# Four interleaved attention layers: projections on two row halves that swap PSUM banks, activations turned by DMA, A's queries read from PSUM, x by way of DRAM

## The chip, the cores and the metric

One core of one Trainium2 chip runs the whole program. The metric is device time in microseconds of one execution; the times shown are three executions and their median. The engines of the core run their own queues in order: TensorE (PE, with its weight loads PEld), VectorE (DVE), ScalarE (ACT), GpSimd (POOL) and SyncE (SP), which here only issues DMAs.

## What is computed

A sequence of 2048 rows of 512 numbers goes through four attention layers, A, B, A, B, each with its residual:

```python
x = x + A(layernorm(x)); x = x + B(layernorm(x))
x = x + A(layernorm(x)); x = x + B(layernorm(x))
```

Both layers have 32 heads of 16 numbers, a projection to queries, keys and values (512 to 1536) and an output projection (512 to 512). In A each row attends to 8 keys, its own and those 2, 4, ... 14 rows before. In B each row attends to the 256 rows that end with its own. Softmax is over these keys, with scale 1/4. Everything is float32 in and out.

## The kernel before

**Tiling.** Rows are cut into 8 chunks of 256. For each pair of layers and each chunk, `layer_a` and `layer_b` plan all work of that chunk; the scopes A0 to A15 and B0 to B15 number them (8 chunks, two pairs of layers).

**Numbers.** Projections multiply float32 values as two float16 parts, high and low: every product is three matmuls (high by high, high by low, low by high), on full 128-row tiles, accumulated in float32 in PSUM. `norm` computes mean and variance on DVE, the reciprocal root on POOL, the normalized rows `xn` on ACT; PE turns them by four transposes into the tile `pt`, ACT copies the high part `xh` and DVE subtracts it for the low part `xl`. `proj_t` makes a turned result of 512 by 256 (q and k of both layers, v of A) in two PSUM tiles, one after the other; `proj_n` makes an unturned one (v of B, both output projections), one tile of 128 rows at a time.

**A.** ACT copies q from PSUM to SBUF; DVE (and POOL for some) multiplies it with the shifted keys into `pr`; PE sums over the 16 numbers of a head by a 0/1 matrix, as column tiles, into `L`; softmax in `e`; PE spreads the probabilities over the numbers of a head by `selt`, on 32 rows, into `pb`; DVE multiplies with the values into `pw`, POOL or DVE sums.

**B.** The high and low parts of q and k go through DRAM (`re`) into the stacked tiles `stk`, where a 48-row slice holds one head's three products. `sq` are the scores for the row maxima, `m`; the maxima are split in two float16 parts, turned by PE (`pm`), copied, and put by DMA into two further rows of `stk`, so that `sk`, on 64 rows, gives scores less the maximum. ACT takes the exponential into `p`, POOL masks, PE multiplies with the values as column tiles into `av`; sums, reciprocals and the result's new layout go through DMAs (`os`, `rc`, `scr`, `oc`).

**Memory.** PSUM has two pools: `q_sc`, two tiles of two banks for scores, and `q_pj`, four banks for everything else. The rows x of a chunk stay in SBUF (`px`, three buffers) from A's load to the end of B.

**The order.** Nothing runs in the order of the calls. `plan.add(engine, us, fn, r, w, mode, ...)` records a task; `ORDER[scope]` gives, for each task of a scope in order of recording, its place in the queue of its engine, all scopes together. A negative entry -1-p means place p on the task's other engine (`alt`). `Plan.order` then merges the five queues by the planned costs and writes the program. So the engines' orders are written out in full, and every engine waits at the head of its own queue. `IDLE` tasks (three matmuls without use) stand in PE's order where the plan expects it to run empty.

Of the kernel before, what the change touches and what calls it, by code (L numbers as in the profile page):

```python
# [9 lines left out]
F16 = mybir.dt.float16  # L10
# [8 lines left out]
P = 128  # L19
# [339 lines left out]
}  # L359
IDLE = 110  # L360
LAG = {"PE": 0.23, "DVE": 0.13, "ACT": 0.16, "POOL": 0.1, "SP": 0.0}
RATE = 0.33
SLOW = 0.25
# [165 lines left out]
def kernel(  # L529
# [193 lines left out]

    x_dr = {}
    vx_dr = {}
    x_in = {}
    st8 = {}


    def norm(l, c):  # L730
# [15 lines left out]
        def rstd():  # L746
            nc.gpsimd.tensor_tensor(out=rs.t[:, 0], in0=rs.t[:, 0], in1=mhalf, op=ALU.pow)
# [602 lines left out]
```

## Time and profile before

| | |
|---|---|
| runs | 1522.99, 1513.79, 1518.68 us; median 1518.68 us |
| span of the profiled execution | 1515.1 us; no other time of it is given |
| PE busy, by modelled ends | 1394.5 us, 92% |
| DVE busy | 1257.6 us, 83% |
| ACT busy | 732.5 us, 48% |
| POOL busy | 695.4 us, 46% |
| mean granted clock of PE | 0.959 |
| bytes moved by DMA | 96.34 MB |

The span runs from the first to the last instruction of the execution that was profiled. A group's row gives line, engine, operation, output and inputs with their shapes and count, then busy time in us and the mean of one in ns, then the engine's idle time before them and what ended it. Matmuls overlap, so their durations are longer than their distance; a row of the timeline with its start time shows the distance.

### The profile page before, as it was taken

The numbers are of one execution on the slowest core, as the hardware profiler recorded it, in microseconds if no ns is written. First come the engines' busy times: TensorE is split into PE (matmuls) and PEld (weight loads), VectorE is DVE, ScalarE is ACT, GpSimd is POOL, SyncE is SP. The second block draws the span as 40 slices with busy tenths as digits, with TensorE's granted clock in tenths as the row PEclk, the third lists the DMA queues.
The fourth block names the chain that finished last, engine by engine and source line by source line (L and its number), as shares of the span: only waits on it lengthen the run. The fifth ranks groups of instructions, "written<-read, shape, count | busy, mean of one in ns | idle before, by whom it ended". The sixth has DMA issues, their size and how long they took to land.

```text
span 1515.1 us, 35124 instructions
## 1 busy us (share of the span) xinstructions
PE 1394.5 (92%) x14186; PEld 793.1 (52%) x14186; DVE 1257.6 (83%) x2361; ACT 732.5 (48%) x1011; POOL 695.4 (46%) x783
## 2 busy tenths in 40 slices
PE   6899989989898998989999998999989899898988
PEld 4574636546374553736446363645637365463544
DVE  6968797987979888897988869798897979889774
ACT  6522445455455554455545344544544555445554
POOL 2504163463726356172452727255372735628232
PEclk9898989999999998999999898998999999999999
DMA  6030211222121221222112122212212121121221
GB/s 236 15 97 23 69 47 56 56 61 75 41 87 37 70 56 53 78 52 77 45 52 77 39 87 52 84 38 60 79 41 85 33 88 48 57 77 40 77 53 44
DMA packets 73091, 96.34 MB, mean 64 GB/s; under 512 B 17120, under 2 KB 44256, under 8 KB 72928
## 3 DMA queue, kind: packets, MB, share of 16 engines
q1 hardware_dynamic: 72672, 93.83, 21.5%
q8 instruction: 111, 1.82, 0.5%
q14 instruction: 52, 0.43, 0.1%
q10 hardware_dynamic: 256, 0.26, 0.1%
HBM read 49.81 MB, written 34.05 MB: 55 GB/s over the span
## 4 chain that ended last, share of the span: by engine, by line
PE 56%; DVE 19%; POOL 7%; issue 6%; ACT 5%; DMA 4%; SPq 3%; ACTq 0%; POOLq 0%; DVEq 0%
PE pq L792 9%; PE pq L793 7%; PE pq L794 7%; PE av L1201 6%; DVE m L1117 5%; PE sk L1169 4%; ACT p L1175 4%; PE L L929 3%; DVE sq L1115 3%; PE po L811 3%; PE sq L1096 3%; PE po L813 2%; PE po L812 2%; POOL pw L1008 2%; PE sq L1099 2%
## 5 line engine op out<-in xcount | busy, mean ns | idle before, releaser
L1175 ACT ACTIVATE p<-sk,sclB 128x768 f32<-128x768 f32 x480 | 426.6, 900 | 297.5 <-PE sk L1171 278.3
L1184 POOL TENSOR_SCALAR_AFFINE_SELECT p<-p 128x1024 f32<-128x1024 f32 x240 | 266.6, 1116 | 499.4 <-ACT p L1175 455.5
L1117 DVE TENSOR_REDUCE m<-sq 128x2 f32<-128x512 f32 x448 | 310.4, 693 | 15.4
L1115 DVE COPY_PREDICATED sq<-maskt,sq 128x256 f32<-128x256 int16 x448 | 188.8, 421 | 81.4 <-PE sq L1099 74.7
L1201 PE MATMUL av<-p,v 128*32 128x128 f32 (+1 forms) x3840 | 202.6, 334 | 7.4 <-POOL p L1184 7.3
L921 DVE TENSOR_TENSOR pr<-kv,q 128x512 f32<-128x512 f32 x223 | 167.4, 807 | 35.4 <-ACT q L900 17.1
L1169 PE MATMUL sk<-stk,stk 64*128 64x256 f16 x960 | 138.2, 287 | 36.8 <-DVE m L1117 20.2
L1201 PEld LDWEIGHTS av<-p,v 128*32 128x32 f32 x3840 | 109.0, 110 | 93.7 <-issue 33.3
L1001 DVE TENSOR_TENSOR pw<-pb,kv 128x1024 f32<-128x1024 f32 x128 | 153.1, 1214 | 4.0 <-POOL o L1010 1.7
L1008 POOL TENSOR_TENSOR pw<-pw 128x512 f32<-128x512 f32 x104 | 132.7, 1276 | 25.1 <-DVE pw L1001 24.4
L1096 PE MATMUL sq<-stk,stk 48*128 48x128 f16 (+1 forms) x896 | 114.5, 255 | 32.0 <-DVE m L1117 17.8
L1099 PE MATMUL sq<-stk,stk 48*128 48x256 f16 (+1 forms) x1024 | 128.4, 252 | 8.5 <-DVE m L1110 3.6
L1169 PEld LDWEIGHTS <-stk 64*128 64x128 f16 x960 | 53.3, 94 | 156.4 <-issue 99.4
L1096 PEld LDWEIGHTS <-stk 48*128 48x128 f16 x896 | 50.0, 95 | 123.1 <-issue 78.8
L1171 PE MATMUL sk<-stk,stk 64*128 64x128 f16 x960 | 109.3, 223 | 0.0
L763 ACT ACTIVATE xn<-x,rs 128x512 f32<-128x512 f32 x64 | 52.0, 813 | 80.9 <-DVE rs L750 72.9
L1009 POOL TENSOR_TENSOR pw<-pw 128x256 f32<-128x256 f32 x104 | 76.3, 734 | 8.2
L921 POOL TENSOR_TENSOR pr<-kv,q 128x512 f32<-128x512 f32 x33 | 46.5, 1415 | 58.7 <-PE L L929 36.0
L929 PE MATMUL L<-pr,sel 128*32 128x512 f32 x512 | 70.6, 601 | 0.9 <-DVE pr L921 0.7
L792 PE MATMUL pq<-xh,wA0h 128*128 128x256 f16 x256 | 70.9, 277 | 0.4 <-DVE el L1032 0.4
L792 PE MATMUL pq<-xh,wB0h 128*128 128x256 f16 x256 | 70.2, 274 | 1.0 <-DVE el L1032 1.0
L792 PE MATMUL pq<-xh,wA2h 128*128 128x256 f16 x256 | 70.6, 276 | 0.0
(183 smaller groups left out, 3159.9 us busy)
## 6 DMA issues: line engine op xcount, KB each, us to landing
stk<-re SPq DMA_DIRECT2D x256, 96.0 KB
re<-eh SPq DMA_DIRECT2D x128, 128.0 KB
re<-el SPq DMA_DIRECT2D x64, 128.0 KB
oc<-os SPq DMA_DIRECT2D x120, 64.0 KB
os<-scr SPq DMA_DIRECT2D x15, 512.0 KB
x<-in_A_x_dram SPq DMA_DIRECT2D x8, 512.0 KB
xd<-x SPq DMA_DIRECT2D x16, 256.0 KB
x<-xd SPq DMA_DIRECT2D x8, 512.0 KB
```

The costliest lines, as they stand in the source:

```text
L792: nc.tensor.matmul(ps[mp].t[:, i], wh, xh, start=k == 0, stop=False)
L921: E.tensor_mul(pr.t, window(kv[1].t, m, 64 * tq, 64)[:, 0], qb)
L1001: nc.vector.tensor_mul(pw.t, pb.t.unsqueeze(1).broadcast_to([P, 2, W, 64]), v)
L1008: E.tensor_add(t[:, :, 0:4], t[:, :, 0:4], t[:, :, 4:8])
L1096: nc.tensor.matmul(ps.t[:, par, 0 : (2 - qb) * P], lhs, stk[hf, bef][r, col, qb * P :], start=True, stop=True)
L1099: nc.tensor.matmul(ps.t[:, par, (2 - qb) * P : 3 * P], lhs, stk[hf, now][r, col, : (1 + qb) * P], start=True, stop=True)
L1115: nc.vector.copy_predicated(t[:, :, 0:P], maskt[:, 0:P].bitcast(I16).unsqueeze(1).broadcast_to([P, 2, P]), t[:, :, 2 * P : 3 * P])
L1117: nc.vector.tensor_reduce(out=m.t[:, qb, :, u], in_=t[:, :, 0 : 2 * P], op=ALU.max, axis=AX.X)
L1169: nc.tensor.matmul(o[:, two], k[:, jf * P : (jf + 1) * P], q, start=True, stop=True)
L1175: nc.scalar.activation(pt.t[:, :, 2 * i : 2 * i + 2].rearrange("p s m q -> p m s q"), ps.t[:, :, : 3 * P].rearrange("p m (s q) -> p m s q" ...
L1184: nc.gpsimd.affine_select(out=v, in_=v, pattern=[[0, 8], [-1 if b == 0 else 1, P]], compare_op=ALU.is_gt if b == 0 else ALU.is_ge, fill=0. ...
L1201: nc.tensor.matmul(o, v[:, jj, 17 * h : 17 * h + 32], rhs, start=z == 0 and (b == 0 or first), stop=z == 1 and b == 1, tile_position=(0, 3 ...
```

## The change

- **Projections.** Each matmul over 128 rows becomes two over 64, on the array's upper and lower row half, which write two different PSUM tiles. In a first turn tile 0 takes the upper rows and tile 1 the lower; in a second turn they swap. Between the turns a task on SP, a no-op, waits for the last matmul of the first turn, and the first matmul of the second waits for the no-op (`turn_over`, `turns`). Both tiles of a projection are in use for both turns. There are 8 projections for each of 16 chunk pairs.
- **Turning.** The high part `hi` is taken by ACT from `xn` in SBUF, the low part by POOL or DVE; both are turned by DMA transposes, issued on SP, into `xh` and `xl`. The transposes on PE, their PSUM tiles, and the copies from them go. `rstd` on POOL takes over the small steps of the norm from DVE.
- **A's queries** are not copied; DVE reads them in PSUM. POOL, which doesn't read PSUM here, makes no products any more.
- **A's spreading** matmuls take 64 rows instead of 32, with zeros in `selt` for the other 32.
- **Row maxima of B** are turned as float32 on the two row halves into a tile of `q_sc` (before: split first, turned whole, in `q_pj`); ACT writes the high part, DVE the low.
- **B's values** are accumulated in one tile for each half of a head group, with a copy to SBUF for each.
- **x** is stored to DRAM at the end of A and loaded again for the end of B.
- **ORDER** is new for all scopes, and 16 idle tasks are left of 110.

```diff
 def norm(l, c):
     def stats(t):
         nc.vector.bn_stats(b6.t[:, t], xb.t[:, t])
         nc.vector.bn_aggr(mv.t[:, t], b6.t[:, t])
-        nc.vector.tensor_scalar(rs.t[:, 0, t : t + 1], mv.t[:, t, 1:2], 1.0e-5, 1.0 / (XS * XS), ...)
     def rstd():
+        nc.gpsimd.tensor_scalar(rs.t[:, 0], mv.t[:, :, 1], 1.0e-5, 1.0 / (XS * XS), ...)
         nc.gpsimd.tensor_tensor(out=rs.t[:, 0], in0=rs.t[:, 0], in1=mhalf, op=ALU.pow)
-    def shift():
-        nc.vector.scalar_tensor_tensor(rs.t[:, 1], mv.t[:, :, 0], -1.0, rs.t[:, 0], ...)
+        for t in range(2):
+            nc.gpsimd.tensor_scalar(rs.t[:, 1, t : t + 1], mv.t[:, t, 0:1], rs.t[:, 0, t : t + 1], -1.0, ...)
...
-            plan.add("PE", 0.48, transp, r=[vxn], w=[vpt], mode="F", act=0.213)
-            plan.add("ACT", 0.48, ... nc.scalar.copy(xh.t[:, :, sl], pts.t), r=[vpt], w=[vh])
-            plan.add("DVE", 0.61, ... nc.vector.tensor_sub(xl.t[:, :, sl], pts.t, xh.t[:, :, sl]), ...)
+            def rest(E, xn=xn, hi=hi):
+                E.tensor_tensor(out=xn.t.bitcast(F16)[:, 0:D], in0=xn.t, in1=hi.t, op=ALU.subtract)
+            def turn_h(t=t, hi=hi):
+                nc.sync.dma_start_transpose(xh.t[:, :, t * P : (t + 1) * P], hi.t)
+            def turn_l(t=t, xn=xn):
+                nc.sync.dma_start_transpose(xl.t[:, :, t * P : (t + 1) * P], xn.t.bitcast(F16)[:, 0:D])
+            plan.add("ACT", 0.52, lambda xn=xn, hi=hi: nc.scalar.copy(hi.t, xn.t), r=[vxn], w=[vhi])
+            plan.add("SP", 0.1, turn_h, r=[vhi], w=[vh], size=200)
+            plan.add("POOL", 1.12, rest, r=[vxn, vhi], w=[vlo], mode="S", alt=("DVE", 0.6))
+            plan.add("SP", 0.1, turn_l, r=[vlo], w=[vl], size=200)
+    def turn_over(last, wait, chain):
+        def pause():
+            n = nc.sync.nop(nofuse=True)
+            tc.add_manual_dep(n.ins, last[0].ins.name, SYNC)
+            wait.append(n)
+        v = Val()
+        plan.add("SP", 0.15, pause, r=chain, w=[v])
+        return v
+    def turns(last, wait, ins):
+        if wait:
+            tc.add_manual_dep(ins.ins, wait.pop().ins.name, SYNC)
+        last[:] = [ins]
 def proj_t(l, c, s):
-    def part(mp, i, kk):
-        m = 2 * mp + i
+    def part(turn, i, kk):
         for k in kk:
...
-            nc.tensor.matmul(ps[mp].t[:, i], wh, xh, start=k == 0, stop=False)
-            nc.tensor.matmul(ps[mp].t[:, i], wh, xl, start=False, stop=False)
-            nc.tensor.matmul(ps[mp].t[:, i], wl, xh, start=False, stop=k == 3)
+            for n in range(3):
+                for mp in ((0, 1) if turn == 0 else (1, 0)):
+                    half = (mp + turn) % 2
+                    r = slice(64 * half, 64 * half + 64)
+                    w = wt[T, s, "l" if n == 2 else "h"][r, k]
...
+                    x = d["xl" if n == 1 else "xh"].t[r, k]
+                    turns(last, wait, nc.tensor.matmul(ps[mp].t[:, i], w, x, ...))
...
+    for turn in range(2):
...
+                    plan.add("PE", 0.655, lambda turn=turn, i=i, kk=kk: part(turn, i, kk), act=0.64,
+                             r=[*d["vxt"], vwt[T, s], *chain], w=[*vps, nxt], mode="R")
...
+        if not turn:
+            chain.append(turn_over(last, wait, chain))
 def finish(l, c, o, vo):
+    if T == "B":
+        mid, vmid = x_mid[c]
+        xb = buf("px", [P, 2, D], F32, "x", f"xr{l}_{c}")
+        plan.add("SP", 0.5, lambda: nc.sync.dma_start(xb.t, mid.t.rearrange("(t p) d -> p t d", p=P)), ...)
...
+    if T == "A":
+        plan.add("SP", 0.4, lambda t=t, mid=x_mid[c][0]: nc.sync.dma_start(mid.t[t * P : (t + 1) * P], xb.t[:, t]), ...)
 def layer_a(l, c):
-                if s == 0:
-                    plan.add("ACT", 0.49, ... nc.scalar.copy(q.t[:, m], ps[mp].t), r=[vps], w=[vq[mp]])
+            if s == 0:
+                q, vq = ps, vpss
...
-                    E.tensor_mul(pr.t, window(kv[1].t, m, 64 * tq, 64)[:, 0], qb)
+                    nc.vector.tensor_mul(pr.t, window(kv[1].t, m, 64 * tq, 64)[:, 0], qb)
...
-                        r = slice(64 * th + 32 * a, 64 * th + 32 * a + 32)
-                        nc.tensor.matmul(pbs[a].t, selt[r, g], (half() if z else eh.t)[r], ...)
+                        r = slice(64 * th, 64 * th + 64)
+                        nc.tensor.matmul(pbs[th].t, selt[r, a, g], (half() if z else eh.t)[r], ...)
 def layer_b(l, c):
-            pm = buf("q_pj", [P, 2, P], F16, "pj", f"pm{l}_{c}_{j}")
+            pm = buf("q_sc", [P, 2, 512], F32, "sc", f"pm{l}_{c}_{j}")
...
+            plan.add("PE", 0.15, mrow, r=vm, w=[vpm], mode="R")
+            plan.add("ACT", 0.27, mhigh, r=[vpm], w=[vmt[0]])
+            plan.add("DVE", 0.42, mlow, r=[vpm, vmt[0]], w=[vmt[1]])
...
-                nc.scalar.copy(os_[hf].t[:, 2 * hp : 2 * hp + 2], acc.t)
+                    nc.scalar.copy(os_[hf].t[:, k], acc.t[:, 0])
-IDLE = 110
+IDLE = 16
```

More of the change, by code (lines that the diff above doesn't have):

```diff
@@ L796, in proj_t @@
-        for mp in range(2):
-            chain = []
+                for n in range(3):
+                    for mp in ((0, 1) if turn == 0 else (1, 0)):
+                        half = (mp + turn) % 2
+                        r = slice(64 * half, 64 * half + 64)
+                        m = 2 * mp + i
+                        w = wt[T, s, "l" if n == 2 else "h"][r, k]
+                        if T == "A":
+                            w = w.rearrange("p (g h e) -> p g e h", g=2, e=2)[:, mp, i]
+                        else:
+                            w = w[:, m * P : (m + 1) * P]
+                        x = d["xl" if n == 1 else "xh"].t[r, k]
+                        turns(last, wait, nc.tensor.matmul(
+                            ps[mp].t[:, i], w, x, start=turn == 0 and i == 0 and k == 0 and n == 0,
+                            stop=turn == 1 and k == 3 and n == 2, skip_group_check=True))
@@ L803, in proj_t, with proj_n, part @@
                     chain = [nxt]
+            if not turn:
+                chain.append(turn_over(last, wait, chain))
         return ps, vps
-    def proj_n(T, s, xh, xl, vals, t, ps, vps):
-        def part(k):
-            tk = slice(t * P, (t + 1) * P)
-            wh, wl = wt[T, s, "h"][:, k], wt[T, s, "l"][:, k]
-            nc.tensor.matmul(ps.t, xh.t[:, k, tk], wh, start=k == 0, stop=False)
-            nc.tensor.matmul(ps.t, xh.t[:, k, tk], wl, start=False, stop=False)
-            nc.tensor.matmul(ps.t, xl.t[:, k, tk], wh, start=False, stop=k == 3)
-        chain = []
-        for k in range(4):
-            nxt = Val(ps)
-            plan.add("PE", 0.65, lambda k=k: part(k), act=0.64, r=[*vals, vwt[T, s], *chain], w=[vps, nxt], mode="F")
-            chain = [nxt]
+    def proj_n(T, s, xh, xl, vals, ps, vps):
+        last, wait = [], []
+        def part(turn, k):
+            for n in range(3):
+                for t in ((0, 1) if turn == 0 else (1, 0)):
+                    half = (t + turn) % 2
+                    r = slice(64 * half, 64 * half + 64)
+                    x = (xl if n == 2 else xh).t[r, k, t * P : (t + 1) * P]
+                    turns(last, wait, nc.tensor.matmul(
+                        ps[t].t, x, wt[T, s, "l" if n == 1 else "h"][r, k], start=turn == 0 and k == 0 and n == 0,
+                        stop=turn == 1 and k == 3 and n == 2, skip_group_check=True))
+        chain = []
+        for turn in range(2):
+            for k in range(4):
+                nxt = Val(ps[0])
+                plan.add("PE", 0.65, lambda turn=turn, k=k: part(turn, k), act=0.64,
+                         r=[*vals, vwt[T, s], *chain], w=[*vps, nxt], mode="R")
+                chain = [nxt]
+            if not turn:
+                chain.append(turn_over(last, wait, chain))
@@ L1074, in layer_b @@
             os_[hf] = buf("pos", [P, 4, C], F32, "os", f"os{l}_{c}_{hf}")
-        vos = {hf: [Val(os_[hf]), Val(os_[hf])] for hf in range(2)}
+        vos = {hf: [Val(os_[hf]) for _ in range(4)] for hf in range(2)}
         for j in range(4):
@@ new lines, in layer_b, with mrow, rows, cols @@
+            vpm, vmt = Val(pm), [Val(mt), Val(mt)]
+            def mrow(m=m, pm=pm):
+                for qb in range(2):
+                    for th in range(2):
+                        r = slice(64 * th, 64 * th + 64)
+                        nc.tensor.transpose(pm.t[0:8, th, 64 * qb : 64 * qb + 64], m.t[r, qb].rearrange("p a u -> p (a u)"), idf[r, r])
+            def rows(pm=pm):
+                return pm.t[0:8, :, 0:P].rearrange("p h (q x) -> p q h x", q=2)
+            def cols(z, mt=mt):
+                return mt.t[:, z].rearrange("p (q h x) -> p q h x", q=2, h=2)
@@ L1147, in layer_b, with mput @@
+            for z in range(2):
+                def mput(z=z, hf=hf, hp=hp, mt=mt):
+                    nc.sync.dma_start(stk[hf, 0][48 + z : 113 + z : 64, 4 * hp : 4 * hp + 4], mt.t[:, z])
+                plan.add("SP", 0.65, mput, r=[vmt[z]], w=[vst[hf, "m", hp]], size=4)
             for hq in range(2):
                 hh = 2 * j + hq
+                if not final or hq == 0:
+                    acc = buf("q_pj", [P, 2 if final else 1, C], F32, "pj", f"av{l}_{c}_{j}_{hq}")
+                    vacc, chain = Val(acc), None
@@ L1206, in layer_b, with evict @@
                     chain = nxt
+                def evict(k=2 * hp + hq, hf=hf, acc=acc):
+                    nc.scalar.copy(os_[hf].t[:, k], acc.t[:, 0])
+                if not final:
+                    plan.add("ACT", 0.29, evict, r=[vacc], w=[vos[hf][2 * hp + hq]])
             if final:
@@ L1280 @@
     plan.begin("pA")
+    ones = buf("ps1", [P, 2, 64], F32, "rc", "ones")
+    vones = Val(ones)
+    plan.add("POOL", 0.2, lambda: nc.gpsimd.memset(ones.t, 1.0), w=[vones])
     prep("A")
```

197 lines of the change are left out of this document (109 added, 88 removed), and 602 rows, old and new, of the table ORDER.

## The prediction

> **What bounds the kernel now.** I read the page first: its span, the busy times and the chain of waits.
>
> ```profile
> span 1515.1 us, 35124 instructions
> PE 1394.5 (92%) x14186; PEld 793.1 (52%) x14186; DVE 1257.6 (83%) x2361; ACT 732.5 (48%) x1011; POOL 695.4 (46%) x783
> PE 56%; DVE 19%; POOL 7%; issue 6%; ACT 5%; DMA 4%; SPq 3%; ACTq 0%; POOLq 0%; DVEq 0%
> ```
>
> PE has the most work and most of the chain; DVE comes second, ACT and POOL are half idle. A steady stretch, from the view of busy time by windows (PE, PEld, DVE, ACT, POOL, clock, DMA share, GB/s):
>
> ```profile
> 240.00:330.00 90.00, 84.39 (x896) 47.12 (x895) 78.76 (x134) 45.00 (x62) 44.31 (x47) 0.98 0.22 61
> ```
>
> PE is covered for 84 of 90 us there and DVE for 79. So PE time that is taken away counts nearly in full at first, and DVE is close behind. What PE spends it on shows in its rows in order of time (start, duration):
>
> ```profile
> 702.87 0.27 PE L793 MATMUL pq<-xl,wB1h 128*128 128x256 f16 x1
> 702.98 0.27 PE L794 MATMUL pq<-xh,wB1l 128*128 128x256 f16 x1
> 703.19 0.28 PE L1169 MATMUL sk<-stk,stk 64*128 64x256 f16 x2
> 703.31 0.22 PE L1171 MATMUL sk<-stk,stk 64*128 64x128 f16 x2
> 703.36 0.27 PE L1169 MATMUL sk<-stk,stk 64*128 64x256 f16 x2
> 703.47 0.22 PE L1171 MATMUL sk<-stk,stk 64*128 64x128 f16 x2
> ...
> 700.26 0.27 PE L1099 MATMUL sq<-stk,stk 48*128 48x256 f16 x2
> 700.46 0.28 PE L792 MATMUL pq<-xh,wB1h 128*128 128x256 f16 x1
> ```
>
> Durations overlap here; starts tell the pace. A projection matmul (128 rows, 256 columns) is followed after 0.11 us by the next, but after 0.21 us by a score matmul on 64 rows; back from scores to a projection it is 0.20 us instead of 0.11. Changing the form in which the array is used therefore costs about 0.095 us each way. Two score matmuls on the two row halves run as a pair: 0.11 to 0.12 us for a pair of 256 columns, as long as one full matmul.
>
> **The change, part by part.**
>
> **Forms.** Before, projections use 128 rows, A's spreading matmuls 32 rows, scores 64 rows, and the attention values, A's sums and the row maxima column tiles. Pairing each entry of the written-out order with the planned tasks gives PE's order: it changes form 1379 times in the layers (768 of them between projections and scores, 123 to or from the spreads). In the new order all but values and sums run on 64 rows, and 480 changes are left. 899 x 0.095 us = 85 us less on PE. That is a bound from above only in that a change which falls into a wait costs nothing today.
>
> **Turning by DMA.** The transposes on PE go:
>
> ```profile
> 707.70 0.27 PE L794 MATMUL pq<-xh,wB0l 128*128 128x256 f16 x1
> 707.81 0.60 PE L767 MATMUL pt<-idf,xn 128*128 128x128 f32 x4
> 708.25 0.27 PE L792 MATMUL pq<-xh,wB0h 128*128 128x256 f16 x1
> ...
> L767 PE MATMUL pt<-idf,xn 128*128 128x128 f32 x256 | 41.8, 287 | 6.4 <-ACT xn L763 6.3
> ```
>
> Four take 0.44 us from start to the next start, and there are 64 fours: 28 us less on PE. In their place stand 128 DMA transposes of 128 KB on SP's queue, which no row shows; nearest is the put of a 128 KB half (next fence): 0.60 us to issue, and SP then waited up to 1.6 us for it, so about 2.2 us to landing. The chain from xn to xl becomes copy, subtraction, DMA instead of PE, copy, subtraction: about 2 us later for each of 32 norms. I take nothing for that, since the new order issues the turns during the projections of the chunk before and xh, xl have two buffers; without that cover it is 32 x 2.2 = 70 us.
>
> By the Trainium skill ("DMA: Bandwidth & Descriptors", the table under Why a DMA increments its semaphore by 16 and not by 1, column of earlier generations) a transposing DMA between SBUF addresses costs the sequencer 262,144 cycles for 8,192 tiles; by my estimate from its tile of 16 by 128 and 1.2 GHz, one of these would hold SP for 0.85 us, 109 us of SP in all, and the sum would be longer only as far as PE waits for SP; no run here shows it yet.
>
> **Two row halves.** Each projection matmul becomes two on 64 rows that write different banks, so twice the instructions.
>
> ```profile
> L792 PE MATMUL pq<-xh,wA0h 128*128 128x256 f16 x256 | 70.9, 277 | 0.4 <-DVE el L1032 0.4
> L811 PE MATMUL po<-wA3h,oh 128*128 128x512 f16 x128 | 58.0, 453 | 0.1
> ```
>
> There are fifteen groups like the first and nine like the second: 3840 + 1152 = 4992 matmuls that become pairs. The score pairs above keep the pace of one full matmul; their second start lies some ns behind the first. Between 0 and 4 ns a pair, 0 to 20 us; I take 2 ns, 10 us more.
>
> The Trainium skill ("TensorE: Matmul & The Clock Gate", Part 3, The mechanism) says that a weight load overlaps running matmuls only where the row group differs; by that rule row halves would save a weight load per matmul, hundreds of us. The trace differs: full projections already follow each other after 0.11 us with their loads hidden, so the sum gets nothing from it.
>
> **The swap.** Half way each projection swaps banks: PE's last matmul, then a no-op on SP that waits for it, then PE's next. What such a hop costs:
>
> ```profile
> 701.67 0.27 PE L794 MATMUL pq<-xh,wB1l 128*128 128x256 f16 x1
> 701.98 0.60 ACT L1029 ACTIVATE eh<-pq 128x512 f16<-128x512 f32 x1 [0.68 <-PE pq L794]
> ...
> 291.19 0.69 DVE L1117 TENSOR_REDUCE m<-sq 128x2 f32<-128x512 f32 x1
> 291.94 0.28 PE L1096 MATMUL sq<-stk,stk 48*128 48x256 f16 x2 [0.58 <-DVE m L1117]
> ...
> L1042 SPq DMA_DIRECT2D re<-eh x128: 518/600/1873, 90.2 to 1425.6; - x128
> L1042 SPq EVENT_SEMAPHORE  x38: 17/17/17, 90.1 to 1423.5; - x38
> ...
> SPq L1042 <- ACT eh L1029: 100.3, 21, 11.8
> SPq L1053 <- DMA re<-el: 15.1, 16, 1.6
> ```
>
> 0.27 us for the matmul, 0.04 to another engine, 0.02 on SP, 0.06 back to PE: 0.39 us from start to start instead of 0.11, so 0.28 us. There are 8 projections x 16 chunks = 128 swaps. In PE's new order nothing stands between the halves of 10, one task of 19, two or more of 99; a score task is 0.17 us (703.19 to 703.36). Left bare: 10 x 0.28 + 19 x 0.11 = 5 us, the lower end. But SP works in order, and the no-op is queued among its DMA issues; behind it on PE is everything. One issue ahead of each swap would be 128 x 0.60 = 77 us. SP issues five scattered kinds 816 times, some 490 of 1515 us, a third of the time: I take a third of the upper end, 26 us.
>
> **DVE, POOL, ACT.**
>
> ```profile
> L921 DVE TENSOR_TENSOR pr<-kv,q 128x512 f32<-128x512 f32 x223 | 167.4, 807 | 35.4 <-ACT q L900 17.1 <-ACT kv L902 10.8 <-PE L L929 6.2
> L921 POOL TENSOR_TENSOR pr<-kv,q 128x512 f32<-128x512 f32 x33 | 46.5, 1415 | 58.7 <-PE L L929 36.0 <-ACT q L900 10.8 <-ACT kv L902 9.3
> L953 DVE TENSOR_TENSOR e<-L,mx 128x512 f32<-128x512 f32 x14 | 9.7, 692 | 0.5
> L773 DVE TENSOR_TENSOR xl<-pt,xh 128x512 f16<-128x512 f32 x64 | 43.8, 689 | 21.6 <-ACT xh L772 20.0
> L744 DVE TENSOR_SCALAR rs<-mv 128x1 f32<-128x1 f32 x64 | 9.8, 154 | 2.2
> L750 DVE SCALAR_TENSOR_TENSOR rs<-mv,rs 128x2 f32<-128x2 f32 x32 | 11.6, 362 | 7.3 <-POOL rs L747 7.1
> L1126 DVE TENSOR_SCALAR mh<-m 128x16 f16<-128x16 f32 x64 | 24.5, 383 | 1.1
> L1127 DVE SCALAR_TENSOR_TENSOR mh<-m,mh 128x16 f16<-128x16 f32 x64 | 20.0, 313 | 2.2
> L1140 DVE COPY mt<-pm 16x256 f16<-16x256 f16 x64 | 17.4, 272 | 4.7 <-PE pm L1131 4.5
> L1006 DVE TENSOR_REDUCE o<-pw 128x128 f32<-128x1024 f32 x24 | 46.1, 1921 | 0.3
> L900 ACT COPY q<-pq 128x512 f32<-128x512 f32 x32 | 18.7, 586 | 54.8 <-PE pq L794 54.3
> L1236 ACT COPY os<-av 128x512 f32<-128x512 f32 x60 | 35.1, 584 | 54.5 <-PE av L1201 54.2
> ```
>
> Products with queries from PSUM: all 256 on DVE, at the 0.692 us of L953, which also reads PSUM: 177 us instead of 167 (+10), and POOL loses 46.5. Rest of x: 34 of 64 stay on DVE, 43.8 to 23 (-21). The small norm steps move to POOL (-21). Row maxima: 62 us become 128 small subtractions at 0.27 to 0.31 us, 37 (-25). The order puts 36 instead of 24 sums on DVE (+23) and 15 scalings of oc fewer (-13); small remainders +3. Together -44 us on DVE. As DVE is 19% of the chain, I count 8 us of it. POOL gains about what it loses, ACT loses 18.7 and gains some 25 in the split evictions and row maxima: both half idle, no time. Sending x through DRAM adds 48 plain DMAs whose work hides under other traffic (DMA share 0.22); the reload is wanted only behind B's output projection. The 110 idle matmul tasks, now 16, only fill gaps: nothing.
>
> **The sum:** 1515.1 - 85 - 28 + 10 + 26 - 8 = 1430 us. The span lies 3.6 us under the runs' median of 1518.68, well inside their 9 us spread; I leave the forecast at 1430 us.
>
> **The rivals.**
>
> **DVE becomes the bound.** Its 1257.6 us become 1213, and its idle time, 1515 - 1257 = 258 us, stays because it waits for softmax and DMA chains as now: 1471 us, call it 1475. For it: 79 of 90 us covered already; two of four projection banks are held by queries during A's products, so PE can't always fill in. Against: part of DVE's idle time is waiting for PE. Chance 0.17.
>
> **SP holds PE up (the other side).** Each swap stands behind a DMA issue that itself waits: the waits view shows SP held up to 11.8 us at one put. The point from which it decides: 85 us are gained, so 0.66 us more a swap, just over one issue, takes it all. At 0.2 + 1.0 us a swap: 1430 + 128 = 1558 us; transposes that hold SP longer than 0.6 us work the same way. For it: nearly every no-op follows an issuing entry in SP's order. Against: SP is free two thirds of the time. Chance 0.15.
>
> **More is won.** PE's waits shrink too, since the queues run further ahead without forms to change, and turning late costs nothing: swaps at 5 us, pairs at 0, and the 6 uncovered of 90 us halved, 50 us: 1515 - 85 - 28 + 5 - 8 - 30 to 50 = about 1360 to 1385. Chance 0.12.
>
> **It does not do what it says.** The halves of a projection run one after another: 4992 matmuls more at 0.11 to 0.22 us, some 670 us, near 2100. The score pairs speak against it. Chance 0.02. That gains and losses cancel within 0.5%, which is about what a measurement of this kernel tells from no change: 0.04.
>
> **How the numbers follow.** Forecast 0.50, its own range 1390 to 1465 us (swaps from 5 to 77 us, pairs 0 to 20, half of the turning delay). The range of 8 in 10 takes in DVE's case and the better one: 1375 to 1510 us; outside lie SP's case and the tails. Faster: 0.50 + 0.17 + 0.12 = 0.79; same 0.04; slower 0.15 + 0.02 = 0.17.
>
> **What would show it.** Right: score and projection starts 0.11 us apart without the 0.2 us steps; pairs of pq 64x256 at 0.11 us; no pt rows; PE waits for SP below 30 us in total; DVE near 1213 us. Wrong: long PE waits put down to SP or to the turning DMA; pairs well above 0.12 us; products far from 0.69 us; a lower granted clock than 0.98 in steady stretches.

## The result: slower

The changed kernel takes 1652.87 us (median of 4 runs, 1650.77 to 1656.0) against 1518.13 us of the kernel before on the same chip: ratio 1.0884, with a 95% interval of 1.0858 to 1.091. The forecast of 1430 us was wrong by 223 us, and on the wrong side. The profiled execution's span is 1654.3 us.

From the page of the changed kernel, the span, the busy times and the chain of waits by engine:

```profile
span 1654.3 us, 44873 instructions
PE 1331.5 (80%) x18768; PEld 819.5 (50%) x18768; DVE 1197.1 (72%) x2204; ACT 735.8 (44%) x1103; POOL 684.0 (41%) x851
PE 14%; DVE 6%; DMA 4%; ACT 3%; SPq 3%; POOL 2%; issue 2%; ACTq 0%; POOLq 0%; DVEq 0%
```

Every engine has less to do or as much as before: PE 63 us less, DVE 60 us less. PE's idle time, span less busy, grew from 121 to 323 us. The time went into waiting. The chain was followed back over only a third of the span this time (its shares add up to 34%), so nothing is read from it. A steady stretch, from the view of busy time by windows (PE, PEld, DVE, ACT, POOL, clock, DMA share, GB/s):

```profile
240.00:330.00 90.00, 73.82 (x1104) 46.55 (x1098) 70.20 (x121) 40.36 (x62) 41.28 (x51) 0.98 0.33 88
```

PE was covered for 84.4 of these 90 us before and DVE for 78.8; now 73.8 and 70.2. The granted clock here is 0.98 in both, so the steady part isn't slower by its clock.

What PE does is faster, as foreseen. Its rows in order of time (start, duration), the x2 being the pair on the two row halves:

```profile
699.77 0.27 PE L824 MATMUL pq<-xl,wA0h 64*128 64x256 f16 x2
699.88 0.27 PE L824 MATMUL pq<-xh,wA0l 64*128 64x256 f16 x2
699.99 0.27 PE L1233 MATMUL sk<-stk,stk 64*128 64x256 f16 x2
700.10 0.22 PE L1235 MATMUL sk<-stk,stk 64*128 64x128 f16 x2
...
682.70 0.27 PE L824 MATMUL pq<-xh,wB0l 64*128 64x256 f16 x2
682.90 1.51 PE L1265 MATMUL av<-p,v 128*32 128x256 f32 x32
```

A pair starts 0.11 us after the pair before it, a score pair 0.11 us after a projection pair (0.21 before), and only the step to the values, whose form differs, still takes 0.20. DVE's products, sums and small subtractions have the durations that were taken for them:

```profile
L978 DVE TENSOR_TENSOR pr<-kv,pq 128x512 f32<-128x512 f32 x256 | 158.6, 682 | 47.2 <-PE pq L824 33.4 <-ACT p L1239 7.6 <-POOL p L1248 3.1
L1063 DVE TENSOR_REDUCE o<-pw 128x128 f32<-128x1024 f32 x36 | 69.4, 1928 | 0.6
L1197 DVE SCALAR_TENSOR_TENSOR mt<-pm,mt 8x128 f16<-8x128 f32 x128 | 30.2, 271 | 57.7 <-ACT mt L1193 57.4
```

What was not in the trace before is the DMA transpose. SP's rows by source line (shortest, median, longest issue in ns, first and last start in us), and PE waiting for what they bring:

```profile
L773 SPq DMA_TRANSPOSE xh<-xm x64: 1188/1260/2042, 29.5 to 1535.0; - x64
  PE pq L824: 24.8, 14
...
L776 SPq DMA_TRANSPOSE xl<-xn x64: 1188/1216/2423, 25.1 to 1536.4; - x64
  PE pq L824: 23.0, 22
...
L1099 SPq DMA_DIRECT2D re<-eh x128: 517/592/1356, 120.9 to 1556.5; - x128
```

A transpose holds SP for 1.19 us at the least and 1.2 to 1.26 us at the median, twice a put of the same 128 KB (0.59). By the medians, 128 of them take 64 x 1.260 + 64 x 1.216 = 158 us of SP. PE waits 24.8 + 23.0 = 48 us for their results. The packets, from the page before and the page after:

```profile
DMA packets 73091, 96.34 MB, mean 64 GB/s; under 512 B 17120, under 2 KB 44256, under 8 KB 72928
```

```profile
DMA packets 151723, 130.53 MB, mean 79 GB/s; under 512 B 87521, under 2 KB 114657, under 8 KB 151521
```

Packets under 512 B grew from 17 to 88 thousand. The waits of the changed kernel (engine and line, what is waited for: us in total, times, longest):

```profile
PE sk L1233 <- ACT p L1239: 32.5, 63, 2.0
PE pq L824 <- SPq L791: 28.4, 20, 4.5
PE pq L824 <- DMA xh<-xm: 24.8, 14, 11.1
PE sq L1152 <- ACT p L1239: 24.5, 51, 2.1
...
PE po L850 <- SPq L791: 7.5, 5, 2.7
...
PE pv L850 <- SPq L791: 3.6, 3, 1.8
...
SPq L791 <- PE pq L824: 155.1, 40, 16.4
SPq L791 <- PE po L850: 133.5, 24, 31.4
```

PE waits for the no-ops (L791) for 28.4 + 7.5 + 3.6 = 40 us, more than the 30 us that the prediction named as the most if it was right. SP stands at them for 155 + 134 us and more until PE has got there, and whatever is queued behind them waits too. Whether that costs anything is for a run to say.

### The profile page after: what moved, and what is told of

Same layout as the page of the kernel before. It is cut to its first block, busy times and chain, and to the rows that moved or that the text cites. A ratio compares the mean times of both kernels' runs of the same rounds, so it can differ in the third digit from the quotient of the medians.

```text
span 1654.3 us, 44873 instructions
## 1 busy us (share of the span) xinstructions
PE 1331.5 (80%) x18768; PEld 819.5 (50%) x18768; DVE 1197.1 (72%) x2204; ACT 735.8 (44%) x1103; POOL 684.0 (41%) x851
## 2 busy tenths in 40 slices
DMA packets 151723, 130.53 MB, mean 79 GB/s; under 512 B 87521, under 2 KB 114657, under 8 KB 151521
## 5 line engine op out<-in xcount | busy, mean ns | idle before, releaser
L978 DVE TENSOR_TENSOR pr<-kv,pq 128x512 f32<-128x512 f32 x256 | 158.6, 682 | 47.2 <-PE pq L824 33.4
L1152 PE MATMUL sq<-stk,stk 48*128 48x256 f16 (+1 forms) x896 | 119.5, 254 | 56.0 <-ACT p L1239 24.5
L1065 POOL TENSOR_TENSOR pw<-pw 128x512 f32<-128x512 f32 x92 | 117.0, 1272 | 83.7 <-DVE pw L1058 83.5
L1155 PE MATMUL sq<-stk,stk 48*128 48x128 f16 (+1 forms) x1024 | 134.1, 251 | 10.2 <-DVE m L1166 3.9
L824 PE MATMUL pq<-xh,wA0h 64*128 64x256 f16 x512 | 78.6, 273 | 16.9 <-DVE el L1089 11.4
L824 PE MATMUL pq<-xh,wB1h 64*128 64x256 f16 x512 | 74.9, 288 | 19.4 <-DMA xh<-xm 19.3
L824 PE MATMUL pq<-xh,wB0h 64*128 64x256 f16 x512 | 72.4, 279 | 19.3 <-SPq L791 19.3
L1089 DVE SCALAR_TENSOR_TENSOR el<-pq,eh 128x512 f16<-128x512 f32 x64 | 41.9, 685 | 63.0 <-ACT eh L1086 42.8
L824 PE MATMUL pq<-xl,wB1h 64*128 64x256 f16 x512 | 75.1, 289 | 14.9 <-DMA xl<-xn 14.9
L1273 ACT COPY os<-av 128x256 f32<-128x256 f32 x120 | 43.7, 368 | 93.8 <-PE av L1265 93.4
```

The costliest lines, as they stand in the source:

```text
L824: turns(last, wait, nc.tensor.matmul(ps[mp].t[:, i], w, x, start=turn == 0 and i == 0 and k == 0 and n == 0, stop=turn == 1 and k == 3 and ...
L978: nc.vector.tensor_mul(pr.t, window(kv[1].t, m, 64 * tq, 64)[:, 0], qb)
L1065: E.tensor_add(t[:, :, 0:4], t[:, :, 0:4], t[:, :, 4:8])
L1152: nc.tensor.matmul(ps.t[:, par, 0 : (2 - qb) * P], lhs, stk[hf, bef][r, col, qb * P :], start=True, stop=True)
L1155: nc.tensor.matmul(ps.t[:, par, (2 - qb) * P : 3 * P], lhs, stk[hf, now][r, col, : (1 + qb) * P], start=True, stop=True)
```

## The experiments

Times are medians, and each ratio is to the kernel before in the same batch, with its 95% interval.

### Taking the two new dependences out: x1, x3, x4

x1 writes the unturned parts straight into `xh` and `xl`; x3 lets the second turn repeat the halves, without the no-op; x4 does both. The output differs, since x isn't turned or half the sums are missing; order and amount of the other work stay.

```diff
-  nc.sync.dma_start_transpose(xh..., hi.t)      # x1, x4
-  nc.sync.dma_start_transpose(xl..., xn...)     # x1, x4
+  nc.scalar.copy(xh.t[:, :, sl], xn...); E.tensor_tensor(out=xl.t[:, :, sl], ...)
-  for mp in ((0, 1) if turn == 0 else (1, 0)): half = (mp + turn) % 2   # x3, x4
+  for mp in (0, 1): half = mp
-  chain.append(turn_over(last, wait, chain))    # x3, x4
```

> The changed kernel without its 128 DMA transposes: ACT and POOL or DVE write the high and low parts of x, unturned, straight into xh and xl (so the projections read wrong numbers of the right size); every other task keeps its place. Theory 1, the turning: each transpose holds SP for 1.3 us (168 us in all) and all that is queued behind it comes late; without it 1500 to 1560 us instead of 1653. Theory 2, the swap through SP is what costs: still 1600 us or more. Theory 3, the new order and the banks that are held longer cost most: 1600 us or more as well.

> The changed kernel without the swap: the second turn of every projection uses the same row halves as the first (half of the products are made twice, half not at all), so the no-op on SP and the wait for it fall away; matmuls, pairs and places stay. Theory 1 (turning): 1600 us or more, a gain of at most the 40 us that PE is seen to wait for the no-op. Theory 2 (swap): 1560 us or less.

> Both left out, the transposes and the swap. If turning and swap are all that went wrong, 1400 to 1450 us, as forecast or better (1430 less the 26 us put down for the swap). If the new order itself leaves PE and DVE waiting (theory 3): 1490 us or more.

Measured: x1 1549.34 us, 1.0187 (1.0158 to 1.0215); x3 1648.74, 1.0826 (1.0793 to 1.0859); x4 1542.6, 1.0141 (1.0119 to 1.0162). Turning by DMA costs 1652.87 - 1549.34 = 104 us (106 from x3 to x4, which ran in one batch), three quarters of the loss. The swap costs 7 us without turning (x1 to x4, one batch). With turning it costs 4 us by the times (1652.87 - 1648.74) and 9 us by the two ratios, which stem from two batches. So SP's long stands at the no-op are nearly free. The theories of turning and swap don't have what is left: with both gone the kernel is still 22 us slower than the kernel before in its batch. Only the third theory, the new order, allowed for that.

### Holding SP without anybody waiting: x2

x1, with a transpose of the same size put back at each of the 128 places in SP's queue, from a weight tile into a tile that nobody reads.

```diff
+  plan.add("SP", 0.1, lambda: nc.sync.dma_start_transpose(held, wt["A", 0, "h"][:, 0]), r=[vwt["A", 0]])
```

> As the first, but SP issues a DMA transpose of a weight tile at each of the 128 places, into a tile that nobody reads. SP is held as in the changed kernel, but nothing waits for a transpose to land and SP waits for no x. If holding SP is the cost: near the changed kernel, 1600 to 1650 us. If the way through the turn (waiting for x, landing, only then the projection) is the cost: near the run without transposes, 1500 to 1560 us.

```profile
L778 SPq DMA_TRANSPOSE held<-wA0h x64: 1188/1257/2137, 29.8 to 1497.8; - x64
```

Measured: 1614.33 us, 1.0617 (1.0593 to 1.064), 65 us above x1. So 65 of the 104 us come though nobody needs a result. The other 39 come with two waits that x2 doesn't have: PE's for the results (48 us by its waits) and SP's for the rows that are to be turned (54 us for `xn` at L773 alone). x2 moves as many packets as the changed kernel (151,722), so by its time alone the 65 us hold SP's lost time and the traffic together. The traces point to SP. ACT writes `eh` anew only when the put has read its old rows. These waits of ACT, first in x1, then in x2, are:

```profile
ACT eh L1083 <- DMA re<-eh: 7.9, 3, 3.8
...
ACT eh L1083 <- DMA re<-el: 0.9, 1, 0.9
```

```profile
ACT eh L1083 <- DMA re<-eh: 29.0, 6, 7.1
ACT eh L1083 <- DMA re<-el: 17.1, 4, 5.9
```

They grow from 9 to 46 us. SP's own waits for such a put to land don't grow: 12.8 + 10.7 us in x1, 10.2 + 13.0 us in x2. Nor do the packets of the other transfers take longer: one of 2 KB, their most frequent size, took 84 ns at the median in both traces. So the puts go out late: the one of `el` is issued 3.8 us after its rows are written in x2, and 2.0 us in x1, at the median by the traces. The tiles behind them stay taken, and with them the PSUM that they are filled from: PE's wait for DVE to empty a projection tile into `el` grows from 1.2 to 21.5 us. A run with the traffic but without the hold wasn't made, so this is read from the traces and not shown by a run.

### Does PE time count? y1, y2, y3

The kernel before in its own order: y1 lacks the low-weight product for k = 2 and 3 of every projection (832 matmuls), y2 the predicated copy for the first 128 rows of a chunk, y3 both; the output lacks these terms.

```diff
-  nc.tensor.matmul(ps[mp].t[:, i], wl, xh, start=False, stop=k == 3)
+  if k < 2: nc.tensor.matmul(ps[mp].t[:, i], wl, xh, start=False, stop=False)
...
+  if qb:                                          # y2
       nc.vector.copy_predicated(t[:, :, 0:P], ...)
```

> The kernel before, in its own order, without the product of low weights and high rows for k = 2 and 3 of every projection: 640 matmuls of 0.109 us and 192 of 0.216 us fewer, about 111 us of PE busy time; nothing else is changed, and the result lacks these products. The prediction's premise, that PE time taken away counts nearly in full: 1518 - 111 = about 1407 us (1400 to 1430). The rival, that the order makes the other engines' results arrive when they did, so that PE waits for them instead: 1470 to 1510 us, with PE's idle time up by most of what its busy time loses. Run x4, in which some 120 us of PE work are gone and the time is 22 us longer, speaks for the rival, but its order is another one; here the order stays.

> The kernel before, in its own order, without the predicated copy that masks the scores of a chunk's first 128 rows in B (about 94 us of DVE busy time); the result lacks this mask. If PE sets the time, as the prediction has it: 1505 to 1518 us. If DVE does: 1425 us. If the two alternate along the order, so that each sets a part: 1460 to 1500 us.

> Both of these left out together. If PE alone sets the time: as without the PE work alone. If each of the two covers for the other, the gain of both together is larger than the sum of the two gains: 1330 to 1400 us. If the order and the latencies between engines set it: above 1430 us.

The busy line of y1:

```profile
PE 1309.8 (88%) x13354; PEld 715.1 (48%) x13354; DVE 1256.1 (84%) x2361; ACT 729.5 (49%) x1011; POOL 692.6 (47%) x783
```

Measured, with 1520.5 us before: y1 1489.49 us, 0.9804 (0.9755 to 0.9852); y2 1500.93, 0.9871 (0.984 to 0.9903); y3 1467.6, 0.9651 (0.9624 to 0.9678). y1's PE is busy for 1394.5 - 1309.8 = 85 us less, and the time falls by 31 us: 37% of it. (By the distance of starts the 832 matmuls were 111 us, as the expectation has it; then it is 28%.) y2 takes 83.5 us from DVE (1257.6 on the page before, 1174.1 on its own) and gains 20 us: 23%. y3's 53 us are about the sum of 31 and 20. So no engine sets the time by itself, and neither covers for the other; that the two take turns along the order is how I read it. A PE that is busy for 92% of the span is not a PE whose time counts in full.

### What the row halves bring, and what the two tiles cost: x5, x6

x4, with each pair put back as one matmul over 128 rows (x5: both tiles in use from first task to last; x6: one tile after the other). x isn't turned, as in x4.

```diff
-  r = slice(64 * half, 64 * half + 64)
-  matmul(ps[mp].t[:, i], w[r, k], x[r, k])        # a pair, on mp 0 and 1
+  matmul(ps[mp].t[:, i], w[:, k], x[:, k])        # x5: k = kk[turn]; x6: mp = turn
```

> The kernel without DMA transposes and without the no-op between the turns (run x4), in the same order, with every pair of 64-row matmuls of a projection put back as one matmul over 128 rows; both PSUM tiles are still taken from the first task to the last. As in x4, x isn't turned, so the result is another one. It isolates the term 'forms', -85 us. If those 85 us of PE count in full: 1543 + 85 = about 1628 us. If PE time counts as it did where PE work was left out of the kernel before (28% of 111 us): 1543 + 24 = about 1567 us. If a change of the array's form costs nothing here: 1543 us.

> As x5 (128-row matmuls, x not turned), but the first turn's tasks make the whole first tile and the second turn's the whole second, as in the kernel before: the first tile is read while the second is being made, and the second is needed only then. If the two tiles that a projection now holds through both turns are what keeps x4 above the kernel before: 20 us or more below x5. If the PSUM tiles are no limit: as x5, within 5 us.

Measured: x5 1577.66 us, 1.0385 (1.0348 to 1.0422); x6 1573.28, 1.0356 (1.0317 to 1.0396). The halves bring 1577.66 - 1542.6 = 35 us where the sum had 85, 41% of it. The size of the work saved on PE was about right: counted in the traces by the shape of one matmul and the next (128 rows, 48 or 64, 32, column tiles), PE changes form 1545 times in x5 and 616 times in x4, and 929 x 0.095 us = 88 us. Its busy time on the pages falls from 1360.8 to 1300.5 us, 60 us, of which 35 are 58%: more than y1's 37% by the same measure, and still far from all. In this order, holding both tiles costs nothing that can be told from none.

### What the order is worth: w0, v4, w3

The tasks stay as they are; their places in the queues are found anew by one search of equal length. In the planned costs the put of `re` goes from 0.45 to 0.6 us, and a transpose in w3 from 0.1 to 1.28 us. A task that may run on either of two engines can change its engine with its place: w0 has 2383 instructions on DVE instead of 2361 and 753 on POOL instead of 783, and in v4 and w3 a few move as well. To this extent the expectations' "every instruction as it was" is not exact. w0 is the kernel before, v4 is x4 (x not turned, halves not swapped), w3 the changed kernel.

```diff
-ORDER = {"pA": [1, 0, 2, 1, ...], ...}
+ORDER = {"pA": [1, 0, 2, 1, ...], ...}   # other places, all scopes
```

> The kernel before, every task and every instruction as it was, with only the places of the tasks in the engines' queues found anew (its lists of places are other ones), the DMA issues taken at the 0.61 us that the trace shows of them. If the order found before is as good as an order can be, or an order's worth is lost in the durations that vary: 1510 to 1530 us. If the order is part of what sets the time: 1470 to 1500 us, which would be faster than both kernels; then part of any difference between before and after belongs to the order and not to the tasks.

> Run x4 (x not turned, halves not swapped, so another result) with only the places of its tasks in the engines' queues found anew, by the same search and for as long as for run w0; no instruction is added or taken away. If the 22 us by which x4 was slower than the kernel before come from its order: as w0 gained 37 us, x4 gains that and the 22, and its 94 us less PE busy time counts again: 1440 to 1465 us, below w0's 1483. If they come from the tasks (what waits for what, and how long a PSUM tile is held): it gains about what w0 gained, 1495 to 1515 us, and stays above w0.

> The changed kernel, every instruction as it is, with only the places of the tasks found anew, the transposes taken at the 1.3 us that they hold SP by the trace instead of 0.1. If the loss is only that the order didn't reckon with SP being held: below 1500 us. If part of it is the order and part the hold itself: 1540 to 1590 us. If an order can't help, since SP is what is short: above 1620 us.

Measured: w0 1483.0 us, 0.9752 (0.9705 to 0.9798), faster than both kernels; v4 1508.6, 0.9923 (0.9896 to 0.995); w3 1589.67, 1.0449 (1.0411 to 1.0486). The same search gains 37 us on the kernel before, 34 on x4 and 63 on the changed kernel, so the changed kernel's order lost some 26 to 29 us more than the two others. It reckoned 0.1 us for a transpose, which is the likely reason. But the hold isn't ordered away: w3 is still 81 us above v4 (turning and swap together), where the old orders had 110. And x4's tasks stay 22 to 26 us above those of the kernel before in both pairs of orders, the old ones and those of this search.

### Idle matmuls: y4, y5, z1, v5

The traces put most of x4's loss at the beginning of the program: A's first product with the values (`pw`) starts at 50.9 us in the kernel before and at 70.2 us in x4, 19 of the 27 us by which x4's profiled span is longer. Busy time in the first 100 us and from 1450 to 1515 us, in the kernel before and then in x4 (which goes on to 1542.5):

```profile
0.00:100.00 100.00, 81.28 (x571) 56.02 (x572) 73.27 (x148) 54.27 (x82) 29.54 (x57) 0.95 0.36 110
1450.00:1515.00 65.00, 54.19 (x664) 28.57 (x664) 38.02 (x73) 31.27 (x38) 22.85 (x21) 1.00 0.18 49
```

```profile
0.00:100.00 100.00, 53.33 (x464) 28.50 (x465) 66.02 (x130) 46.37 (x69) 29.35 (x63) 0.87 0.33 106
1450.00:1515.00 65.00, 50.84 (x664) 24.16 (x664) 42.64 (x82) 34.73 (x48) 22.50 (x21) 0.87 0.25 67
```

The clock is 0.95 and 1.00 there before, 0.87 and 0.87 in x4. The idle matmuls lie just there, and in x4, where 48 of 330 are left, most of them themselves run at the slow pace (median 406 against 273 ns):

```profile
L1310 PE MATMUL idle<-selt,idh x330: 269/273/421, 14.1 to 1511.4; 128*128 128x256 f16 x165
```

```profile
L1375 PE MATMUL idle<-selt x48: 269/406/421, 25.6 to 72.3; 128*128 128x256 f16 x48
```

y4 leaves them out of the kernel before; y5, z1 and v5 put 94 idle tasks back into x4, the changed kernel and v4, in gaps of PE's queue at both ends.

```diff
-  for _ in range(3): nc.tensor.matmul(junk.t, idh, selt...)   # y4: none
-IDLE = 16
+IDLE = 110                                                    # y5, z1, v5, with places in "W"
```

> The kernel before, in its own order, with the 110 idle tasks issuing no matmul (330 matmuls without use are left out). The prediction took the idle tasks at nothing. If that holds: 1518 us. If they keep the granted clock up where PE waits at the beginning and the end of the program (its clock is 0.90 to 1.00 there, in the kernels with 48 idle matmuls 0.75 to 0.87): the clock of these stretches falls and the time rises by 15 to 30 us, to 1533 to 1548 us.

> Run x4 (x not turned, halves not swapped) in its own order, with 94 idle tasks put back, 110 in all as in the kernel before: 72 of them in gaps of PE's queue in the first 260 us, 22 in the last 130. If missing idle matmuls are why x4 loses 19 us before its first A values and 8 after the last: 1543 us falls to 1518 to 1530 us, and the clock of the first 100 us rises from 0.87. If idle matmuls are worth nothing, or stand in the way of what PE waits for: 1543 us or more.

> The changed kernel, correct as it is, in its own order, with 94 idle tasks put back in the same manner. By the theory of the clock 10 to 25 us are won: 1628 to 1643 us. If the idle matmuls are worth nothing: 1653 us.

> Run v4 (x4's tasks in an order found anew) with 94 idle tasks put back in the same manner. By the theory of the clock v4's 25 us above w0, which has 110 idle tasks, go: 1509 us falls to 1480 to 1492 us. If idle matmuls are worth nothing and it is the tasks: 1509 us.

Measured: y4 1533.86 us, 1.0089 (1.0058 to 1.012); y5 1535.35, 1.0099 (1.0062 to 1.0136); z1 1656.18, 1.0891 (1.085 to 1.0933); v5 1508.15, 0.9912 (0.9882 to 0.9941). y4's first and last windows:

```profile
0.00:100.00 100.00, 66.10 (x386) 39.55 (x387) 71.35 (x144) 52.32 (x78) 29.04 (x55) 0.81 0.34 106
1450.00:1515.00 65.00, 51.34 (x626) 22.40 (x624) 43.17 (x81) 36.66 (x45) 25.17 (x23) 0.82 0.18 44
```

Without idle matmuls the kernel before loses 14 us and its clock falls to 0.81 and 0.82 at the ends. So the idle tasks are worth 14 us there, not nothing. Put back they bring 7 us to x4 at most (the intervals of x4 and y5 overlap), and none that can be told to the changed kernel or to v4, though y5's clock is 1.00 in its first 100 us, against 0.87 in x4. So a faster clock at the beginning was not what these kernels waited for; for x4 the next section shows what stood there.

### x loaded late: y6, y7

By the traces the changed kernel's order issues the first load of x behind weight loads. The first normalized rows in the kernel before and in x4 (first and last start in us):

```profile
L763 ACT ACTIVATE xn<-x,rs x64: 799/813/823, 9.3 to 1403.6; 128x512 f32<-128x512 f32 x64
```

```profile
L769 ACT ACTIVATE xn<-x,rs x64: 797/812/843, 22.8 to 1422.3; 128x512 f32<-128x512 f32 x64
```

y6 moves that load behind six weight loads in the kernel before; y7 moves it to the front in y5, with the first norm's tasks on DVE and ACT.

```diff
-ORDER["A0"][0] = 0        # y6: SP's place of the first load of x
+ORDER["A0"][0] = 6
-ORDER["A0"][0] = 7        # y7, and the norm's places on DVE and ACT moved ahead
+ORDER["A0"][0] = 0
```

> The kernel before with one place changed: SP issues the first load of x behind six weight loads of 512 KB, about where the changed kernel's order has it, instead of first. By the traces x's statistics begin at 4.7 us in the kernel before and at 16.2 us in x4. If the late load is what makes x4 lose at the beginning: 1519 us rises by 8 to 15 us, to 1527 to 1534 us. If something later hides it (the weights are needed as well): within 3 us of 1519 us.

> Run y5 (x4 with the idle tasks put back) with the first load of x issued first and the first norm's tasks moved ahead to fit in DVE's and ACT's queues; nothing else. If the late load costs 8 to 15 us there: 1535 us falls to 1520 to 1527 us. If the weights, which now come later by as much, hold the first projections up instead: 1535 us or more.

Measured: y6 1527.93 us, 1.0051 (1.0033 to 1.007), 8 us lost; y7 1540.44, 1.0105 (1.0069 to 1.0141), nothing gained on y5's 1.0099. In y7 the rows do come early, but A's first sums don't. y5's and y7's `L` (first and last start):

```profile
L979 PE MATMUL L<-pr,sel x512: 589/593/1062, 47.6 to 1368.9; 128*32 128x512 f32 x171
```

```profile
L978 PE MATMUL L<-pr,sel x512: 589/593/1063, 50.2 to 1378.3; 128*32 128x512 f32 x171
```

The expectation's rival for that, that the weights pushed back hold the first projection up, is not what the trace shows. In y7 the low parts of the rows were written by 16.2 us, and the weights of the first projection (`wA1h`, `wA1l`) were finished by 22.3 us, yet PE starts it at 36.9 us:

```profile
20.99 1.26 DVE L722 SCALAR_TENSOR_TENSOR wA1l<-stk,pscA,wA1h 128x1024 f16<-128x1024 f32 x1
...
36.73 0.27 PE L677 MATMUL pamB<-idf,amB 128*1 128x128 f32 x1 [1.39 <-ACT wB3l L670]
36.93 0.28 PE L816 MATMUL pq<-xh,wA1h 64*128 64x256 f16 x2
```

What stands ahead of it in PE's order are the small matmuls `pamB` that find the scales of B's weights, with idle matmuls between them; the last waits 1.39 us for ACT to be done with a B weight (`wB3l`). x4 has the same order (first projection at 34.8 us, right behind the `pamB` of 34.6). In the kernel before, the first projection starts at 18.2 us and the first `pamB` at 35.8:

```profile
18.24 0.42 PE L792 MATMUL pq<-xh,wA0h 128*128 128x256 f16 x1
```

So y7 couldn't show what an early x is worth. The beginning of x4 is held by the place of `pamB`, and how much of the end that is worth was not tried; v4's order starts its first projection at 22.6 us and keeps its 25 us above w0.

## Why the prediction was wrong, step by step

The prediction's sum was 1515.1 - 85 - 28 + 10 + 26 - 8.

- **"So PE time that is taken away counts nearly in full at first."** This step failed. It was read from a busy share of 84 in 90 us. PE's busy time counted 37% in y1 and 58% in x5, DVE's 23% in y2. The share tells how full an engine is; what its time is worth only a run with less of it tells.
- **Forms, -85 us.** The mechanism was right (0.11 us instead of 0.21 in the trace after), and so was the count: by the shapes in the traces PE changes form 1503 times before and 620 times after (weight scaling and idle matmuls included), 883 fewer where the prediction had 899. The term was mis-sized for the reason above: 35 us of time.
- **Turning by DMA, nothing.** This step failed worst: +104 us. The nearest row, a put at 0.60 us, was half the price (1.19 at the least, 1.22 to 1.26 at the median), and the delay was taken as covered. The upper bound of 32 x 2.2 = 70 us counted only the late result. It left out that 128 issues hold SP for 158 us, with all puts queued behind them, and the 70 thousand small packets; x2 puts 65 us on these two without anybody waiting, and the traces put them on the hold. The Trainium skill's figure ("DMA: Bandwidth & Descriptors", the table under Why a DMA increments its semaphore by 16 and not by 1), set aside there at an estimated 0.85 us, was on the right side of the put's row and still short of the 1.19 us that the trace shows. The Trainium skill also advises TensorE for a 128 by 128 transpose where a PSUM destination will do ("VectorE: DVE Perf Modes", Rules for kernel authors); the rows agree: four such transposes took 0.44 us of PE before, the two DMA transposes in their place take about 2.5 us of SP (1.260 + 1.216).
- **PE's transposes, -28 us.** They went from the trace; their worth was not measured alone.
- **Row halves, +10 us.** Right: pairs start 0.11 us apart. The rival by which they run one after another fell with the same rows. The Trainium skill's rule on weight loads and row groups ("TensorE: Matmul & The Clock Gate", Part 3, The mechanism), which would have made halves faster than full rows, found no support: both paces are 0.11 us.
- **The swap, +26 us.** Right in kind, too dear: 4 to 9 us, near the lower end of its bounds (5 us). One third of an SP issue for each swap was an average; in this order the no-op's wait is mostly SP's. PE waits for it for 40 us by the trace, but leaving the no-op out returned only 4 to 9 of them.
- **DVE, -44 us.** The durations were right; its busy time fell by 60 us, to 1197 instead of 1213. The 8 us counted of it are near y2's 23% (0.23 x 44 = 10). That is luck: they were taken from DVE's 19% of the chain, which says where the chain ran and not what less work is worth.
- **Idle tasks, "only fill gaps: nothing".** Failed: 14 us in the kernel before (y4).
- **The order.** The prediction took the new places as given, and for the turns as early enough. They reckoned with 0.1 us for a transpose, and a search with 1.28 us regains 63 us (w3), 26 more than the kernel before regains (w0). They also put the scales of B's weights ahead of A's first projection, which starts at 34.8 us in x4 instead of 18.2.
- **Two of its sums don't come out.** "More is won" adds up to 1349 to 1369 us, not 1360 to 1385. The forecast's own range, 1390 to 1465, is narrower than the bounds it names: swaps, pairs and half of the turning delay added up give 1399 to 1526 us. The measured time lies outside either way.

Of the rivals, SP's (1558 us, 0.15) had the right engine and side, and its half sentence on transposes that hold SP longer than 0.6 us was the event; but it put the price on the swaps. DVE as the bound fell with y2.

The loss of 135 us then reads: 104 turning, 7 swap, 24 for all else (x4; 22 by the kernel before of its own batch). In that 24, the row halves bring -35 us, the idle matmuls cost about 14 and the late load of x about 8, both as measured on the kernel before (in x4 `pamB` may hide the load). Some 37 us are then left, and what the missing PE transposes and the shorter DVE work should have brought. This rest stays open: taking both causes out of x4 returned 7 us at most (y5, y7; in y7 `pamB` still held the beginning), another order kept the distance at 25 us (v4 against w0), and queries held in PSUM, x by way of DRAM and the row maxima in the score tiles weren't tried one by one.

## What to carry to other kernels

Before work is moved to a queue for the first time, its issue has to be priced as time of that queue and not only as latency, with the number of issues beside it: 128 x 1.2 us on SP cost more than everything that PE saved. Where two engines are each some 80 to 90% busy, a microsecond of busy time taken from one was worth a quarter to three fifths here (y2, y1, x5), so a change that saves PE time alone has to be cheap elsewhere. And an order that was searched for one set of costs should be searched again, for the kernel before as well, before two sets of tasks are compared: w0 does with places alone what the change did not do.

## What the runs showed of the hardware

- A DMA transpose of 128 rows by 512 float16 numbers holds the issuing SP for at least 1.19 us, at the median 1.22 to 1.26, at the longest 2.4; a put of as many bytes 0.52 at the least and 0.59 at the median. x2's transposes from a weight tile agree (1.188, 1.257).
- 128 transposes add 151,723 - 82,089 = 69,634 DMA packets by the pages of the changed kernel and x1, 544 each for 128 KB, nearly all under 512 B.
- Matmuls without use keep the granted clock up at the ends of the program: 0.95 against 0.81 in the first 100 us, 1.00 against 0.82 from 1450 to 1515 us (before, y4). It was worth 14 us there. In x4, whose clock in the first 100 us rose from 0.87 to 1.00 (y5), it was worth 7 us at most, and in v4 nothing that can be told (v5).
